# Gated mix of linear attention and a squared-ReLU network: the query weights folded in the first block, as 32 by 32 array tiles, and kept in DRAM until the second half

## The chip, the cores and the metric

The kernel runs on one core of a Trainium2 chip (trn2). The metric is the device time of one execution in microseconds; times given are medians of several runs. In the profile PE is the matrix engine TensorE (PEld its weight loads), DVE is VectorE, ACT is ScalarE, POOL is GpSimd and SP is SyncE, which only issues DMA transfers. PSUM has eight banks of 128 partitions x 512 float32 values; PE writes its products there.

## The reference

An input x of 2048 rows and 512 columns goes through two branches, mixed by a gate for each row:

```python
g = sigmoid((x * gate_w).sum(-1, keepdims=True))
q, k, v = split(x @ wqkv)                       # 32 heads of 16 columns
pq, pk = q @ w_phi[h], k @ w_phi[h]             # for each head h: 16 x 16
phi(p) = concat(softmax(p), softmax(-p))        # 32 features a head
kv, z = phi(pk).T @ v, phi(pk).sum(rows)
a = (phi(pq) @ kv) / (phi(pq) @ z + 1e-6) @ wo  # attention branch
h = relu(x @ w1 + b1) ** 2                      # 1792 hidden columns
b = h @ w2 + b2
out = g * a + (1 - g) * b
```

Since `q @ w_phi` is linear in x, the kernel multiplies the query weights with the heads' w_phi first, once ("folds" them), and x with the folded weights. It does the same for the keys.

## The kernel before

**Products.** A float32 value is split into a high part in the format float32r and a low part, value minus high (`split`, L62: ACT copies the high part, L64, DVE subtracts, L67). A product of two such numbers takes three matmuls (`mm3`, L75 to L79: high x high on L77, low x high on L78, high x low on L79).

**Order of the work.** `work_list` runs over two halves of the hidden columns (sweep 0 and 1), in each over four blocks of 512 rows, in each over seven chunks of 128 hidden columns: 56 steps. A step makes u = w1 chunk x block for a later step (`up_step`; ACT reads u with its bias and ReLU on L418, squares it on L419 and splits it), and adds its own hidden chunk x w2 chunk into four banks d (`down`). Between these products everything else is placed by a table: `at(slot, f)` (L782 and L785 to L838) puts f at half step `slot`; step t holds the slots 2t to 2t + 1.5. Within a slot, `tc.issue_after` orders an instruction behind another one of its engine, and `tc.high_priority` lets an instruction go ahead of others in its engine's queue where its own inputs allow. The result is one fixed queue for each engine, which the engine works off in order.

**The key and value part (sweep 0).** `load_fold` (L143) loads w_phi and the four 128-row pieces of the key weights into tiles "row" (six buffers, shared with the rows for the gate). `tiles_fold` (L177) multiplies them at half step 5.5 with 32 by 32 tiles of the PE array into the four banks a, b, e and f; DVE turns these (L196), and ACT copies them beside the value weights. The joint weights (keys and values in one 512 x 1024 matrix) are made into the operands of a product scheme with seven products in place of eight (`joint`, L218): DVE makes the sums of weight blocks (L216), `operand` (L203) splits them. Operands 2, 4, 5 and 7 (`HELD`) stay in SBUF, in tiles "wa" (2 and 4) and "wb"; 1, 6 and 3 (`KEPT`) are stored to DRAM by POOL (`wkeep`, L213) and loaded again by ACT's queue for each use (L635). Operand 4 is made last, at half step 14.5 (`joint_last`). Pairs of row chunks go through `block` (L637, matmuls on L647 to L649) from half step 14 on, with sums of blocks of x that DVE and POOL make (`sums_add`, L605).

**PSUM.** u, q, num, att and the folds take their banks from a list (`bank`, L51): the one used longest ago first. It holds a, b, e and f at the start. Bank b leaves the list at half step 6 (in `do_joint`) and holds the sum kv later; e leaves it at half step 14 for the pairs.

**The query weights before.** At half step 49 `do_wT(wqT)` loads w_phi (again) and the four pieces of query weights, 256 KB each (L145, L147). At half steps 53 to 56 `do_fold` makes one 128 x 512 piece k of the folded weights each (`fold`, L150): four float32 matmuls of 128 x 128 x 128 (L154) into one bank, which ACT and DVE split into the tiles "wa". They are due at 56.5, when the first query chunk is projected (`do_q`).

**Gate.** `gate_load` and `gate_chunk` (L259 to L268) load x by rows (L263) and have DVE sum x times gate_w for each row; for block 0 the loads stand at half steps 5.5, 5.5, 7.5 and 9.5, the chunks three half steps later.

Of the kernel before, what the change touches and what calls it, by code (L numbers as in the profile page):

```python
# [35 lines left out]
def tile_gated_mix(ctx: ExitStack, tc: tile.TileContext, xT, xn, wqT, wkT, wphi, wv, wo, w1, b1, w2, b2, gw, out):  # L36
# [96 lines left out]
    wkeep = dram.tile([len(KEPT), 2, P, 2 * D], F32, name="wkeep")  # L133
    zrow = dram.tile([2 * D], F32, name="zrow")
# [8 lines left out]
    def load_fold(wT):  # L143
        t = [row() for _ in range(1 + NK)]
        nc.sync.dma_start(t[0], wphi)  # L145
        for g in range(NK):
            nc.sync.dma_start(t[g + 1], wT[:, g, :])  # L147
        return t

    def fold(loaded, nm, k):  # L150
        wph, *t = loaded
        ps = bank(f"fold{nm}{k}")
        for g in range(NK):
            nc.tensor.matmul(ps[:, g * P:(g + 1) * P], t[g][:, k * P:(k + 1) * P], wph[:, g * P:(g + 1) * P],  # L154
                             start=True, stop=True)
# [47 lines left out]
    def operand(i, j, src, slot=None, ehi=None, elo=None):  # L203
        if i in HELD:
            w, k = "ab"[i > 4], 2 * (HELD.index(i) % 2) + j
            hi, lo = (wpool.tile([P, 512], F32R, tag=f"w{w}{hl}{k}", name=f"w{i}{j}", bufs=1) for hl in "hl")
        else:
            t = st["slots"][slot] if slot is not None else work.tile([P, 2 * D], F32R, tag="tb", name="spare", bufs=2)
            hi, lo = both(t)
        split(src, hi, lo, ehi or nc.scalar, elo or nc.vector)  # L210
        st["W"][i, j] = hi, lo
        if i in KEPT:
            st["stored"] = nc.gpsimd.dma_start(wkeep[KEPT.index(i), j], t.bitcast(F32))  # L213
# [45 lines left out]
    def gate_load(n):  # L259
        eng, pin = ((nc.sync, "in" if n > 1 else "wv"), (nc.gpsimd, "summed"), (nc.sync, "ahead"), (nc.sync, "ahead"))[n // NC]  # L260
        st["xn", n] = row()
        with tc.issue_after(st[pin].ins):
            st["xrow"] = eng.dma_start(st["xn", n], xn[n])  # L263
# [191 lines left out]
    def do_fold(nm, k):  # L455
        with tc.issue_after(st["up"].ins):
            st["wa", nm, k] = fold(st["wT"], nm, k)
        if k == NK - 1:
            st["wa"] = [st["wa", nm, i] for i in range(NK)]
            if nm == "k":  # L460
                banks.pop()
# [328 lines left out]
    for slot, j, piece in ((5.5, 0, 0), (6, 1, 0), (8, 0, 1), (9, 1, 1), (10, 1, 2), (11, 0, 2)):  # L790
        at(slot, do_joint, j, piece)
    for j in range(2):
        at(14.5, joint_last, j)
    for b in range(NB):
        for c in range(NC):
            s = b * SL + 2.5 * c - 1 if b > 1 else 17.5 + c / 2 if b else max(5.5, 3.5 + 2 * c)
            if b != 1 or c < 2:
                at(s, gate_load, b * NC + c)
            at(s + (4.5 if b == 1 else 3), gate_chunk, b * NC + c)
        if c == NC - 1:  # L800
            at(s + 4.5 if b == 1 else s + 3, gates, b)
# [7 lines left out]
    at(49, do_wT, wqT)  # L809
    for k in range(NK):  # L810
        at(53 + k, do_fold, "q", k)
# [137 lines left out]
```

## Time and profile before

| | |
|---|---|
| time, median of 3 runs | 508.11 us (507.98 to 508.29) |
| span of the profiled execution | 506.8 us |
| part of the median outside that span | 1.3 us |
| PE busy | 502.0 us, 99% |
| DVE, ACT, POOL busy | 405.9, 256.2, 88.4 us |
| moved by DMA | 76.13 MB |

The profile is that of one execution. Busy time counts an engine's instructions but not its waits; a row of a timeline gives the start, the duration, the engine, the line, the operation with its output and inputs, and in brackets the idle time ahead of it and what ended that. A matmul of 512 columns shows as 0.39 us, but the next one starts 0.227 us after it, since they are pipelined. A float32 matmul leaves two records, so sixteen instructions are x32.

### The profile page before, as it was taken

To read this page: it belongs to the slowest core of one execution; us is meant where nothing else is said; L and a number is where in the kernel's file an instruction comes from. 1 tells how busy PE (TensorE), PEld (TensorE's weight loads), DVE (VectorE), ACT (ScalarE), POOL (GpSimd) and SP (SyncE) were. 2 spreads that over 40 slices of the span, in tenths; PEclk is the share of its full clock that TensorE was granted. 3 is DMA by queue.
4 is the path that set the end of the run, shared out by engine and by line. 5 is a ranking of instruction groups with operands and counts; after the bars stand their busy time and mean duration, and the time that the engine had idled before them with its cause. 6 is when DMAs were issued, how large, how long until landed. Compare 5 with 4: busy or idle time off the path is not lost.

```text
span 506.8 us, 9362 instructions
## 1 busy us (share of the span) xinstructions
PE 502.0 (99%) x3522; PEld 406.4 (80%) x3522; DVE 405.9 (80%) x679; ACT 256.2 (51%) x458; POOL 88.4 (17%) x103
## 2 busy tenths in 40 slices
PE   9999999999999999999999999999999999999997
PEld 5878788788888888888888877788787878788776
DVE  5569957998795979796898989897869797897824
ACT  4887655555263474454574745444456354333540
POOL 0000151204420025000013050211222221111200
PEclk9999999999999999999999999999999999999999
DMA  8858587756854578771375221325112231032102
GB/s 262 279 194 284 187 311 219 232 196 231 288 187 158 182 236 308 242 228 65 87 219 195 63 83 43 104 76 147 39 31 88 71 85 43 8 125 63 38 26 84
DMA packets 45861, 76.13 MB, mean 150 GB/s; under 512 B 6904, under 2 KB 23032, under 8 KB 45816
## 3 DMA queue, kind: packets, MB, share of 16 engines
q1 hardware_dynamic: 36104, 41.78, 26.7%
q10 hardware_dynamic: 6768, 23.79, 13.7%
q0 software_dynamic: 2944, 9.96, 5.4%
q8 instruction: 28, 0.46, 0.4%
q14 instruction: 17, 0.14, 0.1%
HBM read 57.68 MB, written 11.54 MB: 137 GB/s over the span
## 4 chain that ended last, share of the span: by engine, by line
PE 90%; DVE 6%; DMA 1%; POOL 1%; ACT 1%; issue 1%; DVEq 0%; POOLq 0%; ACTq 0%
PE d L77 9%; PE d L78 9%; PE d L79 9%; PE u L77 9%; PE u L78 8%; PE u L79 8%; PE pX L647 3%; PE att L79 3%; PE pX L649 3%; PE att L77 3%; PE att L78 3%; PE pX L648 3%; PE q L79 2%; PE q L78 2%; PE q L77 2%; PE pY L647 2%
## 5 line engine op out<-in xcount | busy, mean ns | idle before, releaser
L418 ACT ACTIVATE r<-u,b1c 128x512 f32<-128x512 f32 x56 | 38.5, 688 | 125.5 <-PE u L79 123.6
L77 PE MATMUL d<-w2h,hh 128*128 128x512 f32 x222 | 86.9, 391 | 0.0
L78 PE MATMUL d<-w2l,hh 128*128 128x512 f32 x222 | 86.5, 390 | 0.0
L79 PE MATMUL d<-w2h,hl 128*128 128x512 f32 x222 | 86.4, 389 | 0.0
L77 PE MATMUL u<-xh,w1h 128*128 128x512 f32 x212 | 83.7, 395 | 0.0
L78 PE MATMUL u<-xl,w1h 128*128 128x512 f32 x212 | 82.6, 390 | 0.0
L79 PE MATMUL u<-xh,w1l 128*128 128x512 f32 x212 | 82.5, 389 | 0.0
L333 POOL TENSOR_TENSOR ez<-e,z 128x512 f32<-128x512 f32 x32 | 43.1, 1370 | 166.6 <-ACT e L305 166.6
L67 DVE TENSOR_TENSOR hl<-r,hh 128x512 fp32r<-128x512 f32 x56 | 37.7, 674 | 24.7 <-ACT hh L64 24.7
L77 PEld LDWEIGHTS d<-w2h,hh 128*128 128x128 f32 x222 | 41.7, 188 | 9.2 <-issue 0.6
L78 PEld LDWEIGHTS d<-w2l,hh 128*128 128x128 f32 x222 | 41.7, 188 | 8.9 <-DVE w2l L67 0.4
L77 PEld LDWEIGHTS u<-xh,w1h 128*128 128x128 f32 x212 | 39.8, 188 | 11.1 <-issue 2.9
L79 PEld LDWEIGHTS d<-w2h,hl 128*128 128x128 f32 x222 | 41.7, 188 | 8.7
L79 PEld LDWEIGHTS u<-xh,w1l 128*128 128x128 f32 x212 | 39.8, 188 | 8.6 <-DVE w1l L67 0.2
L78 PEld LDWEIGHTS u<-xl,w1h 128*128 128x128 f32 x212 | 39.8, 188 | 7.9
L305 ACT ACTIVATE e<-e 128x1024 f32<-128x1024 f32 x27 | 28.6, 1059 | 25.2 <-DVE e L303 25.0
L308 DVE TENSOR_REDUCE sm<-e 128x64 f32<-128x1024 f32 x27 | 32.8, 1214 | 10.4 <-ACT e L305 10.4
L64 ACT ACTIVATE hh<-r 128x512 fp32r<-128x512 f32 x56 | 35.2, 628 | 1.1
L419 ACT ACTIVATE r<-r 128x512 f32<-128x512 f32 x56 | 35.0, 624 | 0.7
L686 ACT ACTIVATE tmp<-pX 128x512 f32<-128x512 f32 x24 | 14.4, 598 | 31.2 <-PE pX L649 27.6
L371 ACT ACTIVATE phiT<-tb 32x256 f32<-32x256 f32 x64 | 26.4, 412 | 6.1 <-DVE tb L356 5.1
L340 DVE TENSOR_REDUCE dz<-ez 128x64 f32<-128x1024 f32 x16 | 19.4, 1211 | 11.5 <-POOL ez L333 11.5
(184 smaller groups left out, 985.5 us busy)
## 6 DMA issues: line engine op xcount, KB each, us to landing
sloto<-wkeep ACTq DMA_DIRECT2D x30, 512.0 KB, 4.1
in<-in_xT SPq DMA_DIRECT2D x42, 256.0 KB, 4.2
slotez<-wkeep ACTq DMA_DIRECT2D x15, 512.0 KB, 4.6
phiT<-tb SPq DMA_DIRECT2D x192, 32.0 KB, 1.9
in<-in_w SPq DMA_DIRECT2D x23, 256.0 KB, 3.2
part<-row POOLq DMA_DIRECT2D x16, 256.0 KB, 5.2
row<-part SPq DMA_DIRECT2D x16, 256.0 KB, 2.7
out<-row SPq DMA_DIRECT2D x15, 256.0 KB, 2.2
```

The costliest lines, as they stand in the source:

```text
L64: i = nc.scalar.activation(hi, src, AF.Copy)
L67: st["lo"] = elo.tensor_tensor(lo, src, hi.bitcast(F32), ALU.subtract)
L77: nc.tensor.matmul(o, ah[:, sa], bh[:, sb], start=first, stop=False)
L78: nc.tensor.matmul(o, ah[:, sa], bl[:, sb], start=False, stop=False)
L79: return nc.tensor.matmul(o, al[:, sa], bh[:, sb], start=False, stop=last)
L305: nc.scalar.activation(ef, ef, AF.Exp)
L308: nc.vector.tensor_reduce(sm, e3, AX.X, ALU.add)
L333: nc.gpsimd.tensor_tensor(ez[:, hs, :], e3[:, hs, :], zbc[half], ALU.mult)
L371: nc.scalar.activation(dst, src, AF.Copy)
L418: st["relu"] = nc.scalar.activation(r, ps, AF.Relu, bias=b1c[:, fc:fc + 1])
L419: nc.scalar.activation(r, r, AF.Square)
L647: nc.tensor.matmul(ps, h, wh, start=first and j == 0, stop=False, skip_group_check=True)
```

## The change

The query weights are loaded and folded in the first block, beside the key weights' work, and the folded weights, turned by DVE, are kept in DRAM until the second half.

- At half step 5.5 the four pieces of query weights are loaded (the tile with w_phi is kept from the key fold). The first gate load of block 0 stands behind them on SP's queue, the other three at 9.5, the gate chunks at 8.5, 12, 12.5 and 13.
- At 9.5 `query_fold` multiplies with sixteen matmuls, each on one 32 by 32 tile of the array over 512 columns, in all four banks a, b, e and f; each reads a 32-row strip of w_phi and of the query weights. DVE turns each bank with one instruction into the tile "turned", which shares its memory with the held operand 4. Bank b leaves the list here, no longer at 6.
- At 11.5 `query_store` stores the turned weights with four DMAs of POOL to `wfold` in DRAM, in runs of 512 bytes.
- At 49 `query_load` loads four plain 128 x 512 rows from there, and at 53 to 56 `query_split` splits one of them each. The sixteen matmuls of 128 x 128 x 128 are gone.

```diff
     def load_fold(wT):
-        t = [row() for _ in range(1 + NK)]
-        nc.sync.dma_start(t[0], wphi)
+        t = [row() for _ in range(NK)]
+        if "wph" not in st:
+            st["wph"] = row()
+            nc.sync.dma_start(st["wph"], wphi)
         for g in range(NK):
-            nc.sync.dma_start(t[g + 1], wT[:, g, :])
-        return t
-
-    def fold(loaded, nm, k):
-        wph, *t = loaded
-        ps = bank(f"fold{nm}{k}")
+            st["wqT"] = nc.sync.dma_start(t[g], wT[:, g, :])
+        return [st["wph"], *t]
+
+    def held(k):
+        if k < 2:
+            return [wpool.tile([P, 512], F32R, tag=f"wa{hl}{k}", name=f"wa{hl}{k}", bufs=1) for hl in "hl"]
+        if k == 2:
+            st["wa23"] = wpool.tile([P, 4, 512], F32R, tag="wa23", name="wa23", bufs=1)
+        return [st["wa23"][:, 2 * (k - 2) + i, :] for i in range(2)]
+
+    def query_fold():
+        wph, *t = st["wT"]
+        pss = [bank(f"fold{r}") for r in range(4)]
         for g in range(NK):
-            nc.tensor.matmul(ps[:, g * P:(g + 1) * P], t[g][:, k * P:(k + 1) * P], wph[:, g * P:(g + 1) * P],
-                             start=True, stop=True)
-        hi = wpool.tile([P, 512], F32R, tag=f"wah{k}", name=f"w{nm}h{k}")
-        lo = wpool.tile([P, 512], F32R, tag=f"wal{k}", name=f"w{nm}l{k}")
-        with tc.high_priority(offset=AHEAD):
-            split(ps, hi, lo, nc.scalar, nc.vector)
-        return hi, lo
+            for r in range(4):
+                rows = slice(32 * r, 32 * r + 32)
+                with tc.issue_after(st["up"].ins):
+                    st["up"] = nc.tensor.matmul(pss[r][32 * g:32 * g + 32, :],
+                                                wph[rows, g * P + 32 * r:g * P + 32 * r + 32], t[g][rows, :],
+                                                start=True, stop=True, skip_group_check=True)
+        tb = st["qrows"] = wpool.tile([P, 4 * NK, 4, 32], F32, tag="wa23", name="turned", bufs=1)
+        for r in range(4):
+            with tc.high_priority(offset=AHEAD):
+                st["qturned"] = nc.vector.transpose(tb[:, :, r, :], pss[r].rearrange("p (k q) -> p k q", q=32))
+        banks.remove(ps_b)
+
+    def query_store():
+        to = wfold.rearrange("t (c q) (g f) -> g q (t c) f", c=4, g=NK)
+        for g in range(NK):
+            with tc.issue_after(st["stored"].ins):
+                nc.gpsimd.dma_start(to[g], st["qrows"][32 * g:32 * g + 32].rearrange("p k r f -> p k (r f)"))
+
+    def query_load():
+        st["wq"] = [row() for _ in range(NK)]
+        for k in range(NK):
+            nc.sync.dma_start(st["wq"][k], wfold[k])
+
+    def query_split(k):
+        hi, lo = held(k)
+        with tc.issue_after(st["up"].ins), tc.high_priority(offset=AHEAD):
+            split(st["wq"][k], hi, lo, nc.scalar, nc.vector)
+        st.setdefault("wa", []).append((hi, lo))
...
-        eng, pin = ((nc.sync, "in" if n > 1 else "wv"), (nc.gpsimd, "summed"), (nc.sync, "ahead"), (nc.sync, "ahead"))[n // NC]
+        eng, pin = ((nc.sync, "wqT"), (nc.gpsimd, "summed"), (nc.sync, "ahead"), (nc.sync, "ahead"))[n // NC]
         st["xn", n] = row()
-        with tc.issue_after(st[pin].ins):
+        with tc.issue_after(st[pin].ins), tc.high_priority(offset=AHEAD) if n < NC else nullcontext():
...
-        if (j, piece) == (1, 0):
-            banks.remove(ps_b)
...
+    at(5.5, do_wT, wqT)
+    at(9.5, query_fold)
+    at(11.5, query_store)
...
-    at(49, do_wT, wqT)
+    at(49, query_load)
     for k in range(NK):
-        at(53 + k, do_fold, "q", k)
+        at(53 + k, query_split, k)
```

`operand` takes the tiles of operands 2 and 4 from `held` now; nothing else of it changes. Line numbers behind the new functions are larger by 24 to 34: the sums of weight blocks on L216 are L250 after the change, the new matmuls are on L167 and the turns on L173.

Where this lands in the queues is shown at three places. The first is PE at half step 9.5, before: the last products d of the step (d_307 to d_309 are three of the four d banks), and behind them the first of the next u.

```order
L79 MATMUL d_307<-w2h_332,hl 128x512
L77 MATMUL d_308<-w2h_332,hh 128x512
L78 MATMUL d_308<-w2l_333,hh 128x512
L79 MATMUL d_308<-w2h_332,hl 128x512
L77 MATMUL d_309<-w2h_332,hh 128x512
L78 MATMUL d_309<-w2l_333,hh 128x512
L79 MATMUL d_309<-w2h_332,hl 128x512
L77 MATMUL u<-xh_0_526,w1h_130 128x512
```

The same place after (the same d banks are now d_308 to d_310, fold_632 to fold_635 are the four banks of the fold). The last four of the sixteen fold matmuls are shown; twelve like them stand ahead, right behind the product that was the first row above.

```order
L167 MATMUL fold_632<-row 32x512
L167 MATMUL fold_633<-row 32x512
L167 MATMUL fold_634<-row 32x512
L167 MATMUL fold_635<-row 32x512
L77 MATMUL d_309<-w2h_333,hh 128x512
L78 MATMUL d_309<-w2l_334,hh 128x512
L79 MATMUL d_309<-w2h_333,hl 128x512
L77 MATMUL d_310<-w2h_333,hh 128x512
L78 MATMUL d_310<-w2l_334,hh 128x512
L79 MATMUL d_310<-w2h_333,hl 128x512
L77 MATMUL u<-xh_0_533,w1h_131 128x512
L78 MATMUL u<-xl_0_534,w1h_131 128x512
```

The fold comes in between the d products; six d products stay between it and the next u, whose bank is that of fold_632.

The second place is DVE at the same time, before: low parts of operands (sloto, w) and of w2, and sums of weight blocks (raw, tmp).

```order
L67 TENSOR_TENSOR sloto_396<-tmp,sloto_396 128x512
L216 TENSOR_TENSOR raw_398<-raw_400,raw_398 128x512
L216 TENSOR_TENSOR tmp<-tmp 128x512
L67 TENSOR_TENSOR w2l_557<-in,w2h_556 128x512
L216 TENSOR_TENSOR tmp<-tmp 128x512
L67 TENSOR_TENSOR w_583<-raw_398,w_582 128x512
```

After:

```order
L67 TENSOR_TENSOR sloto_397<-tmp,sloto_397 128x512
L250 TENSOR_TENSOR raw_399<-raw_401,raw_399 128x512
L250 TENSOR_TENSOR tmp<-tmp 128x512
L173 STREAM_TRANSPOSE turned<-fold_632 128x16x32
L173 STREAM_TRANSPOSE turned<-fold_633 128x16x32
L173 STREAM_TRANSPOSE turned<-fold_634 128x16x32
L173 STREAM_TRANSPOSE turned<-fold_635 128x16x32
L250 TENSOR_TENSOR tmp<-tmp 128x512
L67 TENSOR_TENSOR w2l_564<-in,w2h_563 128x512
L67 TENSOR_TENSOR w_588<-raw_399,w_587 128x512
```

The four turns stand behind two sums and ahead of the low part of w2.

The third place is PE between half steps 53 and 56, at the second of the four old folds (foldq), before:

```order
L77 MATMUL d_2355<-w2h_384,hh 128x512
L78 MATMUL d_2355<-w2l_385,hh 128x512
L79 MATMUL d_2355<-w2h_384,hl 128x512
L154 MATMUL foldq_2989<-row 128x128 x4
L77 MATMUL u<-xh_0_2041,w1h_2486 128x512
L78 MATMUL u<-xl_0_2042,w1h_2486 128x512
```

After, with the same d bank now d_2390:

```order
L77 MATMUL d_2390<-w2h_385,hh 128x512
L78 MATMUL d_2390<-w2l_386,hh 128x512
L79 MATMUL d_2390<-w2h_385,hl 128x512
L77 MATMUL u<-xh_0_2076,w1h_2521 128x512
L78 MATMUL u<-xl_0_2077,w1h_2521 128x512
```

The four matmuls are gone here and at the other three places; the u products follow the d products directly.

More of the change, by code (lines that the diff above doesn't have):

```diff
@@ L133, in tile_gated_mix @@
     wkeep = dram.tile([len(KEPT), 2, P, 2 * D], F32, name="wkeep")
+    wfold = dram.tile([NK, P, D], F32, name="wfold")
     zrow = dram.tile([2 * D], F32, name="zrow")
@@ L204, in operand @@
         if i in HELD:
-            w, k = "ab"[i > 4], 2 * (HELD.index(i) % 2) + j
-            hi, lo = (wpool.tile([P, 512], F32R, tag=f"w{w}{hl}{k}", name=f"w{i}{j}", bufs=1) for hl in "hl")
+            k = 2 * (HELD.index(i) % 2) + j
+            if i > 4:
+                hi, lo = (wpool.tile([P, 512], F32R, tag=f"wb{hl}{k}", name=f"w{i}{j}", bufs=1) for hl in "hl")
+            else:
+                hi, lo = held(k)
         else:
@@ L453, in do_wT @@
         st["wT"] = load_fold(wT)
[L455 to L461, printed above, removed]
     def do_joint(j, piece):
```

7 lines of the change are left out of this document (4 added, 3 removed).

## Prediction

> **What bounds the kernel now.** I read the page first, then the chain of work that ended last, the groups of instructions by form, and the timelines of PE, DVE, ACT and SP around half step 9.5, where the change puts its work, and around 53 to 56, where it takes work away. From the page:
>
> ```profile
> span 506.8 us, 9362 instructions
> PE 502.0 (99%) x3522; PEld 406.4 (80%) x3522; DVE 405.9 (80%) x679; ACT 256.2 (51%) x458; POOL 88.4 (17%) x103
> PEclk9999999999999999999999999999999999999999
> PE 90%; DVE 6%; DMA 1%; POOL 1%; ACT 1%; issue 1%; DVEq 0%; POOLq 0%; ACTq 0%
> ```
>
> PE is busy for 502.0 of 506.8 us at full granted clock, and the chain runs over PE for 90%. So each microsecond that PE is spared shortens the run, and each one that PE is made to wait lengthens it, unless a wait of PE further on shrinks by as much. The stretches of ten microseconds in which the new work lands look the same; the columns are PE, PEld, DVE, ACT and POOL busy, PE clock, DMA share and KB per us:
>
> ```profile
> 36.00:46.00 10.00, 10.00 (x45) 7.93 (x44) 8.92 (x18) 8.43 (x16) 2.21 (x4) 1.00 0.92 293
> 46.00:56.00 10.00, 10.00 (x46) 8.29 (x45) 10.00 (x20) 6.95 (x13) 1.06 (x2) 1.00 0.49 187
> ```
>
> PE has no gap there, but DVE is nearly full too (8.92, then 10.00 of 10 us). This is where DVE gets four more instructions that PE will wait for.
>
> **Removed: four folds on PE.** In the chain they stand as four pieces at half steps 53 to 56:
>
> ```profile
> 245.55 0.89 PE foldq L154 x8
> 250.63 0.89 PE foldq L154 x8
> 254.25 0.89 PE foldq L154 x8
> 257.88 0.89 PE foldq L154 x8
> ```
>
> All four lie on PE's path with nothing beside them: 4 x 0.89 = 3.56 us less. ACT and DVE still make the four high and low parts there, now from rows in SBUF rather than from PSUM; the count of instructions is the same, the weights are first needed at half step 56.5, and no wait of PE hung on them. I cost this at nothing. The gate chunks of block 0 move by a few half steps; their gates are due only when block 0 ends, and I cost that at nothing too.
>
> **Added on PE: the fold at half step 9.5.** No row shows sixteen 32x32 tiles over 512 columns, so I bound it by the two nearest forms:
>
> ```profile
> L183 PE MATMUL fold<-row 32*32 32x128 f32 x128 | 1.9, 278 | 0.0
> 27.07 1.83 PE fold L183 x104
> 489.94 1.02 PE num L382 x32
> L196 DVE STREAM_TRANSPOSE turned<-fold 128x512 f32<-128x512 f32 x4 | 2.5, 684 | 0.4 <-PE fold L183 0.4
> ```
>
> The key fold has 128 records of 128 columns in 1.83 us. The numerator has 32 records of 256 columns on eight tiles, four records to a tile: 1024 columns in a tile's turn in 1.02 us. The new fold has 16 instructions, 32 records (the old folds too left two records for each instruction), two to a tile, so 2 x 512 = 1024 columns as well. I take 1.0 us from the numerator, which has the same length of run, with 1.8 as the upper end. The size matters little, as the next term shows.
>
> **Added: PE waits for VectorE.** The fold takes all four PSUM banks that the u products rotate through. Where PE stands now:
>
> ```profile
> 39.84 0.39 PE L79 MATMUL d<-w2h,hl 128*128 128x512 f32 x1
> 40.07 0.39 PE L77 MATMUL d<-w2h,hh 128*128 128x512 f32 x1
> 41.43 0.39 PE L77 MATMUL u<-xh,w1h 128*128 128x512 f32 x1
> ```
>
> The fold comes in ahead of the d product of 40.07. Six d products (six starts of 0.227 us, 40.07 to 41.43) follow it, and then the next u, whose bank is the one that the fold filled first. PE can start this u only when DVE has turned that bank. The fold's fourth bank waits in turn for ACT to have read the last u. Here is ACT, then DVE:
>
> ```profile
> 40.63 0.67 ACT L418 ACTIVATE r<-u,b1c 128x512 f32<-128x512 f32 x1
> 42.31 0.63 ACT L64 ACTIVATE w2h<-in 128x512 fp32r<-128x512 f32 x1 [1.01 <-DMA in<-in_w]
> 42.85 0.62 ACT L64 ACTIVATE sloto<-tmp 128x512 fp32r<-128x512 f32 x1
> ```
>
> ```profile
> 43.50 0.69 DVE L67 TENSOR_TENSOR sloto<-tmp,sloto 128x512 fp32r<-128x512 f32 x1 [0.84 <-ACT sloto L64]
> 44.10 0.68 DVE L216 TENSOR_TENSOR raw<-raw,raw 128x512 f32<-128x512 f32 x1
> 44.71 0.69 DVE L216 TENSOR_TENSOR tmp<-tmp 128x512 f32<-128x512 f32 x1
> 45.31 0.69 DVE L67 TENSOR_TENSOR w2l<-in,w2h 128x512 fp32r<-128x512 f32 x1
> ```
>
> ACT frees the fourth bank at 40.63 + 0.67 = 41.30, so the fold ends near 42.4 and the six d near 43.8. But by the order of the program the first turn stands on DVE where the low part of w2 stands now, that is at 45.31. It cannot come sooner, though it is of high priority: ahead of it on DVE is the low part of the slot (43.50), which waits for ACT's high part (42.85), which stands behind the w2 split (42.31), which waits for a load. DVE goes through its queue in order. The first turn thus ends at 45.31 + 0.68 = 46.0, and u starts at about 46.05 in place of 41.43: **4.6 us more on PE**. Any fold that ends by 44.6 (3.3 us past 41.3) gives the same, so its own 1.0 to 1.8 us is hidden. Behind the waiting u on PE stand all further products; behind the turns on DVE stand the low part of w2 and the rest of the weight sums, 4 x 0.61 = 2.4 us later (0.61 is the step from one start to the next in the rows above), but PE, their reader, is 4.6 us later by then.
>
> Bounds on this term. The load that starts the queue is issued late, because its buffer comes free late:
>
> ```profile
> 32.00 5.16 SPq L87 DMA_DIRECT2D in<-in_w  x3
> 36.83 0.33 SPq L87 DMA_DIRECT2D in<-in_w  x1
> 37.25 1.43 SPq L263 DMA_DIRECT2D row<-in_xn  x2
> ```
>
> It is issued at 36.83 and lands at about 42.3, 5.5 us in a full DMA stretch (share 0.92). The two gate loads right behind it go elsewhere with the change; if that lets it land a microsecond sooner, ACT and DVE are a microsecond sooner and the term is 3.6. Upward: the turn writes 16 strips of 32 with gaps between them, and were it to take twice the 0.68 us of a plain one, the term is 5.3.
>
> By the Trainium skill's page "TensorEngine Tiling (Array Packing)", section PSUM Bottleneck, tiling speeds up the products but not the emptying of PSUM, which may then be what limits. That speaks against this change, and the rows agree: 2.5 us for four turns against 1.83 us for the fold. Were the emptying's own pace the limit, u would wait for one turn right behind the fold, 42.4 + 0.7, under the six d products, and the sum would be the quick rival's below; it is the place in DVE's queue that I go by.
>
> **Given back.** Two waits of PE on the chain, for ACT's and DVE's sums of block pairs, go:
>
> ```profile
> 58.14 0.34 PE pX L647
> 58.94 0.42 PE pX L649
> PEld pX L649 <- DVE sl L67: 0.4, 1, 0.4
> PEld pX L647 <- ACT sh L64: 0.3, 1, 0.3
> ```
>
> Their steps are 0.11 and 0.19 us longer than the usual 0.23. PE comes 4.6 us later and DVE 2.4 us later, so DVE and ACT are in time: 0.3 us less.
>
> **Loads and stores.** The four rows of query weights (1.05 MB) go out at about 29, when the key rows have been read, ahead of the w1 and w2 loads of 32.0:
>
> ```profile
> 26.00:36.00 10.00, 10.00 (x165) 8.03 (x164) 5.47 (x9) 8.38 (x26) 0.10 (x1) 1.00 0.57 194
> 30.00:35.00 5.00, 5.00 (x24) 4.14 (x23) 2.66 (x6) 4.65 (x19) 0.00 (x0) 1.00 0.41 151
> in<-in_w SPq DMA_DIRECT2D x4, 256.0 KB, 2.8
> row<-in_wqT SPq DMA_DIRECT2D x4, 256.0 KB, 4.3
> ```
>
> At a full share 194 KB per us becomes 194 / 0.57 = 340, so 1.05 MB is 3.1 us of all DMA engines, and 30 to 35 has 59% of 5 us free, 2.95 us. So the loads nearly fit: I cost them at 0, with 0.75 us as the end if the w loads land a microsecond later. The query rows themselves have till 40 to land, and took 4.3 us each at half step 49. The plain loads at half step 49 replace others of the same size on the same queue, one fewer: nothing.
>
> **The sum.** -3.56 + 4.6 - 0.3 = +0.75, so 506.8 becomes 507.6 in the span. The median of the runs stands 1.3 us above the profiled span; I keep that: **508.9 us**, within 0.2% (1.0 us, about what a measurement of this kernel can tell from no change) of 508.11. The forecast's own range: with 3.6 for the wait, 508.11 - 0.26 = 507.8; with 5.3 for it, 0.75 for the loads and nothing given back, 508.11 - 3.56 + 6.05 = 510.6.
>
> **The rivals.**
> Quick: the turns don't hold PE. That is so if DVE has turned the first bank by about 43.8, when the six d are through, 2.2 us sooner than I have it. Then PE pays the fold and its wait for ACT's bank only: 42.4 - 40.07 = 2.3 at most, 1.0 at least, so -3.56 + 1.0 to 2.3, 505.5 to 506.9, say 506.3. For it: DVE stands 0.84 us idle at 43.5 and ACT 1.01 us at 42.3, both for a load. Against: both idle times together are less than the 2.2 us needed, and three 0.61 us instructions stand between. Chance 0.16.
>
> Loads in the way: the query rows push the w loads back by more than the free 2.95 us, PE waits for w1 or w2 at 33 to 38 and DVE is later besides. Loads of 256 KB that took 2.8 us in the median would take 5.5 as the one at 36.83 does, so 2.7 us late at most; part of it hides in the wait that PE has anyway. 508.9 + 1 to 2.7, say 510.7. Chance 0.08.
>
> Stores that hold ACT (this ends slower): the tile of turned rows has the memory of one held operand, which ACT writes at half step 14.5. The four stores stand on POOL behind the last kept slot. The rows below are POOL's store of that slot, ACT's u of the time, the time to landing of the block-sum loads, and that of the stores of whole rows:
>
> ```profile
> 54.13 0.53 POOL L213 DMA_DIRECT2D wkeep<-slotez  x1 [1.28 <-DVE slotez L67]
> 67.84 0.69 ACT L418 ACTIVATE r<-u,b1c 128x512 f32<-128x512 f32 x1 [2.25 <-PE u L79]
> DMA to landing us min/median/max: 3.9/5.7/5.7
> part<-row POOLq DMA_DIRECT2D x16, 256.0 KB, 5.2
> ```
>
> The slot's store would come at about 54.1 + 2.4 = 56.5, the four issues (0.53 each) be through by 59.2, and ACT want the memory after the u of 67.84, about 71 to 72 with the delay. So the stores have some 12 us. Loads of block sums, whose runs are 512 bytes like these, took 5.7 us at most; stores of whole rows 5.2. From 12 us on ACT stands, and with it the reading of the u and pX banks that PE waits for, up to one for one: at 16 us, 508.9 + 4 = 512.9. Twice the slowest row is under the point where it begins, so chance 0.05. In the Trainium skill, "DMA: Bandwidth & Descriptors", section Specifications, 512 bytes is the smallest transfer at full line rate; these runs just reach it, which would leave this rival out.
>
> Tiles that don't run at once: the fold is hidden up to 3.3 us. At the old folds' pace, 0.89 / 8 = 0.11 us for 128 columns, 32 records of 512 columns one after another take 14 us, 10.9 more than is hidden: 519.8. The key fold's 1.83 us for 128 such tiles speaks against it. Chance 0.03.
>
> **How the numbers follow.** The forecast's mechanism has the remaining 0.68. Of its range, 507.8 to 509.1 is within 0.2% and 509.1 to 510.6 above; I give 0.42 and 0.26, since the point lies at 508.9. Faster by over 0.2%: 0.16, the quick rival. Slower: 0.26 + 0.08 + 0.05 + 0.03 = 0.42. Same: 0.42. The range reaches into both sides: from 506.4, which leaves out about half of the quick rival (0.08), to 510.7, which leaves out the last two rivals and half of the loads (0.12).
>
> **What would show it.** Right: the key line is u's first product behind the new fold, waiting about 2.3 us for DVE's turn, with the fold's fourth bank waiting about 1 us for ACT; u starts at 46 us, the chain passes there from PE to DVE; the four 0.89 us pieces are gone at 245 to 258; no wait on ACT for stores before the operand at 70. Wrong: u starts by 44.5 (quick), or PE shows a wait for w1h or w2h between 33 and 39 (loads), or ACT's copy behind 67 waits for a DMA (stores), or the fold's row is over 3.3 us (tiles).

## The result and the profile after

The changed kernel takes 515.51 us (median of 4 runs, 513.41 to 516.66) where before takes 508.08 (4 runs): a ratio of 1.0142, 95% interval 1.0129 to 1.0155, 7.4 us slower by the medians. The forecast was 508.9 and its range ended at 510.7, so it was wrong: it saw the wait for the turned bank, and missed most of the time. The profiled execution is the shortest of the four, 513.41 us with a granted clock of 1.000; the other three had a clock of 0.995 to 0.996 and took 515.4 to 516.7. So there are two things to explain: 4.8 us in the span (511.6 against 506.8), and the 2.0 to 3.3 us more of the other three executions.

The page of after, its span, busy times and chain:

```profile
span 511.6 us, 9388 instructions
PE 500.9 (98%) x3522; PEld 403.5 (79%) x3522; DVE 406.8 (80%) x683; ACT 257.0 (50%) x458; POOL 90.6 (18%) x107
PE 81%; DVE 10%; DMA 4%; issue 2%; POOL 1%; ACT 1%; SPq 0%; DVEq 0%; POOLq 0%; ACTq 0%
```

PE is busy for 1.1 us less than before, in a longer span, and its share of the chain went from 90% to 81%: PE waits now. What PE waited for (us in total, times, longest), in a kernel that had only 0.18 us of such waits behind its start:

```profile
PE pX L671 <- DMA sloto<-wkeep: 2.4, 1, 2.4
PE u L77 <- DVE turned L173: 1.4, 1, 1.4
PE u L77 <- ACT w1h L64: 1.2, 1, 1.2
PE att L79 <- DVE o L67: 0.8, 1, 0.8
```

Only the second of these four was a term of the forecast's sum. Where they stand on PE, with the fold between them:

```profile
38.03 0.50 PE L77 MATMUL u<-xh,w1h 128*128 128x512 f32 x1 [1.21 <-ACT w1h L64]
41.68 1.75 PE L167 MATMUL fold<-row 32*32 32x512 f32 x32
46.46 0.50 PE L77 MATMUL u<-xh,w1h 128*128 128x512 f32 x1 [1.44 <-DVE turned L173]
66.18 0.50 PE L671 MATMUL pX<-sloto,sh 128*128 128x512 f32 x1 [2.43 <-DMA sloto<-wkeep]
```

The turns on DVE's timeline, and on ACT's the split that waits for w2's load:

```profile
45.70 2.50 DVE L173 STREAM_TRANSPOSE turned<-fold 128x512 f32<-128x512 f32 x4
```

```profile
36.71 0.63 ACT L64 ACTIVATE w2h<-in 128x512 fp32r<-128x512 f32 x1 [1.11 <-DMA in<-in_w]
```

The first turn starts at 45.70 (45.31 forecast) and u at 46.46 (46.05 forecast). To see what each stretch costs, take the start of the same product in both traces; the difference is how late PE is (products whose place in PE's order changed are left out):

| place in after, us | PE later than before, us | what was added there |
|---|---|---|
| 38.0 (u behind the w1 wait) | 1.55 | w1's load behind the query rows |
| 43.4 (d behind the fold) | 3.3 | the fold and its wait for ACT |
| 46.5 (u behind the turn) | 5.0 | the wait for DVE |
| 63.4 (pX) | 4.5 | 0.5 given back |
| 66.2 (pX on the reloaded slot) | 7.0 | a reload |
| 242 | 7.4 | |
| 273 | 3.7 | the four old folds, 3.6, are gone |
| 325, and to the end | 4.6 | a wait for o |

The last two rows belong together. o is the attention's numerator of the first query chunks, and its low part stands in DVE's queue behind steps that need POOL's products with z, the sum of the key features. The first of these products starts at 267.84 in before and waits for ACT there. After the change it starts 5.71 us later and waits for z, which goes through DRAM:

```profile
273.55 2.53 POOL L367 TENSOR_TENSOR ez<-e,z 128x512 f32<-128x512 f32 x2 [8.40 <-DMA z<-zrow]
```

### The profile page after: what moved, and what is told of

The parts are those of the page before. It is cut to its first block, busy times and chain, and to the rows that moved or that the text cites. A ratio compares the mean times of both kernels' runs of the same rounds, so it can differ in the third digit from the quotient of the medians.

```text
span 511.6 us, 9388 instructions
## 1 busy us (share of the span) xinstructions
PE 500.9 (98%) x3522; PEld 403.5 (79%) x3522; DVE 406.8 (80%) x683; ACT 257.0 (50%) x458; POOL 90.6 (18%) x107
## 4 chain that ended last, share of the span: by engine, by line
PE 81%; DVE 10%; DMA 4%; issue 2%; POOL 1%; ACT 1%; SPq 0%; DVEq 0%; POOLq 0%; ACTq 0%
PE d L78 8%; PE d L77 8%; PE d L79 8%; PE u L77 7%; PE u L79 7%; PE u L78 7%; PE pX L671 3%; PE att L79 3%; PE att L77 3%; PE att L78 3%; PE pX L673 3%; PE pX L672 3%; PE q L79 2%; PE q L78 2%; PE q L77 2%; PE pY L673 2%
```

## The experiments

Each was compared with before in runs of its own on the same chip; a median is followed by its difference from that of before beside it. Medians of different chips are compared by these differences. A trace is one execution, and executions of one kernel differ: in the traces here PE is between 0.5 us ahead of before's and 0.2 us behind at 12 us, where no edit has done anything yet.

**The changed kernel again.** No edit.

> The changed kernel as it is, run again beside the others. Ledger theory: the profiled span is again near 511.6 us, 4.8 above before, made up of 1.4 (w1's load behind the query rows) + 1.75 (fold) + 1.7 (turn) - 0.5 (waits given back) + 2.9 (a reload of a kept operand behind the stores of the folded weights) - 3.6 (old folds) + 0.7 (a wait for o at 310 us). Executions with a granted clock under 1.000 are some 2 us longer. Rival: the waits differ from execution to execution, and the profiled one is not typical; then other waits stand in this trace.

514.81 us (+6.0; ratio 1.0133, 1.0101 to 1.0165), clocks 0.993 to 1.000. The same waits stand in its trace: 2.5 us for the reload, 1.8 for the turn, 1.0 for w1. They belong to the kernel, not to one execution. But the profiled one took 513.5 us in the span, 1.8 more than the first, with a clock of 1.00 for as long as PE had products; it has a wait of 1.0 us for the features of a chunk and one of 0.8 us that the profile explains by nothing ("issue"), which the first didn't have. So a lower clock is not the only thing that makes executions differ.

**The stores earlier.**

```diff
-    at(11.5, query_store)
+    at(9.5, query_store)
```

> The four stores of the folded weights stand on POOL ahead of the last two kept slots, so they go at 48 to 52 us, when the DMA engines are nearly idle. Ledger theory: PE's wait of 2.4 us for the reload at 58 to 66 us goes, and the time falls by 2.0 to 2.9 us. Rival (the reload is late because VectorE, and so the stores of the two kept slots, are 2.8 us later): the wait stays, since those two stores come no sooner, and the time falls by less than 0.5 us.

513.16 us (+4.4; ratio 1.0098, 1.0078 to 1.0118), 1.65 less than the changed kernel beside it; the two intervals overlap a little, so it is the trace that decides. First the changed kernel: POOL's stores of the last two kept slots and of the folded weights, then the piece of its chain for the reload that ACT issued at 58.35, and the landing times of the four stores.

```profile
55.09 0.53 POOL L247 DMA_DIRECT2D wkeep<-spare  x1 [9.69 <-DVE spare L67]
55.69 0.53 POOL L247 DMA_DIRECT2D wkeep<-slotez  x1
56.22 2.63 POOL L180 DMA_DIRECT2D wfold<-turned  x4
```

```profile
58.35 7.79 DMA sloto<-wkeep
```

```profile
DMA to landing us min/median/max: 5.0/6.8/8.1
```

2 MB of stores start between 55.1 and 58.9, and the reload of 512 KB right behind them is 7.8 us under way, 4.1 in the median of before. With the four stores at 48 us, PE's waits are:

```profile
PE u L77 <- DVE turned L173: 1.6, 1, 1.6
PE pX L671 <- DMA sloto<-wkeep: 0.3, 1, 0.3
```

The reload's wait is gone, though the two stores of kept slots come as late as ever (54.9 and 55.5). It is the folded weights' stores that hold the reload. The gain in the median is a little under the 2.0 us expected.

**The loads behind w1 and w2.**

```diff
         for g in range(NK):
-            st["wqT"] = nc.sync.dma_start(t[g], wT[:, g, :])
+            with tc.issue_after(st["in"].ins) if "in" in st else nullcontext():
+                st["wqT"] = nc.sync.dma_start(t[g], wT[:, g, :])
...
-    at(5.5, do_wT, wqT)
+    at(6.5, do_wT, wqT)
```

> The four loads of query weights stand on SP behind the loads of w1 and w2 of that step, no longer ahead of them. Ledger theory: PE's wait of 1.2 us for w1 at 38 us goes, but as PE then stands longer at the turn (VectorE is only some 0.5 us sooner), the time falls by only 0.4 to 0.9 us. Rival (the whole queue of ACT and VectorE is late by that load): the turn comes 1.2 us sooner as well and the time falls by 1.2 us or more.

518.79 us (+10.0): worse by 4, which neither theory had. The wait for w1 is gone, but ACT stands at the next thing that shares the DMA engines with the query rows, the store of a kept slot, whose memory ACT wants to write; PE then waits for ACT and longer for the turn:

```profile
42.21 0.63 ACT L64 ACTIVATE sloto<-raw 128x512 fp32r<-128x512 f32 x1 [2.63 <-DMA wkeep<-sloto]
```

```profile
PE fold L168 <- ACT r L453: 2.2, 1, 2.2
PE u L77 <- DVE turned L174: 1.9, 1, 1.9
```

And the granted clock falls behind these waits. The columns are the stretch, PE, PEld, DVE, ACT, POOL, PE clock, DMA share, KB per us:

```profile
46.00:48.00 2.00, 0.19 (x1) 0.00 (x0) 2.00 (x5) 2.00 (x4) 0.53 (x1) 1.00 0.99 331
48.00:50.00 2.00, 1.95 (x7) 1.56 (x8) 2.00 (x4) 0.18 (x1) 0.00 (x0) 0.78 0.72 290
50.00:52.00 2.00, 2.00 (x6) 1.58 (x5) 2.00 (x4) 0.63 (x1) 0.00 (x0) 0.50 0.02 6
52.00:54.00 2.00, 2.00 (x9) 1.57 (x8) 2.00 (x5) 1.26 (x2) 0.00 (x0) 0.87 0.47 133
```

Behind the idle stretch the clock is at one half for 3.4 us (49.1 to 52.5), and once more for 3.4 us at 69.6, behind a wait of 2.2 us for the reload. Three of the four executions have a mean clock of 0.993 and took 518.5 to 519.5 us; the one with 1.000 took 515.23. So two such falls cost 3.3 to 4.3 us here, and without them the edit is about as slow as the changed kernel. This is the second half of the result.

**The fold in two halves.** Two banks at a time, so that the u between them has a bank that needs no turn.

```diff
-        pss = [bank(f"fold{r}") for r in range(4)]
+        two = (2 * half, 2 * half + 1)
+        pss = {r: bank(f"fold{r}") for r in two}
...
-    at(9.5, query_fold)
+    at(9.5, query_fold, 0)
+    at(10.5, query_fold, 1)
```

> The fold is cut in two: row strips 0 and 1 into two banks at half step 9.5, strips 2 and 3 into two banks at 10.5, so that the u between them has a bank that needs no turn. Ledger theory: PE's wait for the turn (1.4 us) and for ACT's read of the last bank (0.4 us) goes, the time falls by 1.5 to 1.9 us, less what the second switch to small tiles costs. Rival (the waits only move: the u after next needs the first half's bank, and VectorE is as late there): the time falls by under 0.5 us. Rival (switching the array to small tiles and back is what costs): the fold's two pieces take longer together than the one piece of 1.75 us, and the time rises or stays.

516.16 us (+7.4), no better. At its place it did what it should: each half takes 1.09 us on PE, no wait for the turn is left, and PE is 2.4 us late at 50 us, not 5.2; 0.7 us of that difference was there at 12 us already, so the halves gain about 2.0. But the reload takes it all back, and the clock goes down behind that:

```profile
PE pX L675 <- DMA sloto<-wkeep: 3.9, 1, 3.9
```

```profile
66.00:68.00 2.00, 2.00 (x7) 1.55 (x6) 0.75 (x1) 1.14 (x2) 0.00 (x0) 0.54 0.93 363
68.00:70.00 2.00, 2.00 (x7) 1.59 (x6) 0.00 (x0) 0.00 (x0) 1.68 (x3) 0.60 0.88 328
```

**Both.** Halves, and the stores pinned behind the store that stood last before the fold, at 10.5.

> Both edits that helped at their own place at once: the fold in two halves (PE is 2.3 us late behind it in place of 5.1), and the stores of the folded weights in the idle stretch before the last kept slots. Ledger theory: with the reload no longer late, the halves' 2.75 us are kept, so the profiled span is 511.0 (stores early alone) - 2.75 = 508.3 us, 1.0 to 1.8 above before, and the granted clock is 1.00 in all executions, since no wait of PE over 1.5 us is left. Rival (another fixed point, such as the gate or the sums of row blocks, holds PE at about 70 us as the reload did): over 510 us.

512.4 us (+4.6; span 509.0, clocks 0.999 to 1.000). That is better than the halves alone (+7.4), but no better than the stores earlier alone (+4.4); the profiled execution, 510.82, is the shortest of four. PE still waits 2.1 us for the reload: the pin moved only the first two of the four stores ahead of the kept slots (48.4), the other two went at 54.3, and the reload was 6.9 us under way.

**Without the query loads.** As the last, with `at(5.5, do_wT, wqT)` taken out.

> The kernel of the halves with early stores, without the four loads of query weights: the fold reads the key rows again, so the query branch gets wrong weights. It prices the loads in the first block. Ledger theory: PE's waits between 33 and 40 us go and the span falls by 0.3 to 1.3 us against the halves with early stores. Rival (the loads cost nothing once the turn isn't waited for): within 0.2 us of it.

511.78 us (+4.0; span 508.7). PE is 0.55 us less late at 50 us, and 0.04 us less at the end. In these two traces the loads have a price at their place, and it is hidden later.

**Before without its folds.**

```diff
-        ps = bank(f"fold{nm}{k}")
-        for g in range(NK):
-            nc.tensor.matmul(ps[:, g * P:(g + 1) * P], t[g][:, k * P:(k + 1) * P], wph[:, g * P:(g + 1) * P],
-                             start=True, stop=True)
+        ps = t[k]
```

> The kernel before with its four folds left out: the query rows are split as they were loaded, so the query branch gets unfolded weights. It measures the most that taking the folds from there can bring. Both theories of the forecast: 3.56 us less than before, 503.2 to 503.8 in the profiled span if before is 507.0. Rival (DVE or POOL sets the time around 250 to 310 us, so part of it is given back): 2 to 3 us less.

505.36 us (-2.4; ratio 0.994, 0.9921 to 0.9959). That is 2.1 to 4.0 us less by the interval, which doesn't leave out the 3.56; the trace does, for its execution: PE is 3.57 us early at 296 us and 2.52 at 325, so one microsecond of the removed folds is worth nothing there. Here is POOL's first product with z and the first attended product that waits, for before, then without the folds:

```profile
267.84 2.53 POOL L333 TENSOR_TENSOR ez<-e,z 128x512 f32<-128x512 f32 x2 [4.18 <-ACT e L305]
305.82 0.50 PE L79 MATMUL att<-woh,o 128*128 128x512 f32 x1 [0.18 <-DVE o L67]
```

```profile
265.31 2.54 POOL L330 TENSOR_TENSOR ez<-e,z 128x512 f32<-128x512 f32 x2 [7.19 <-DMA z<-zrow]
303.30 0.50 PE L79 MATMUL att<-woh,o 128*128 128x512 f32 x1 [1.23 <-DVE o L67]
```

POOL's product moves by 2.53 us and the attended product by 2.52: from there on DVE and POOL set the pace, and POOL now waits for z, which is summed by PE right behind the first of the four folds and then goes through DRAM. Three of the four folds stood behind that point, so leaving them out doesn't bring z.

**The same with z from elsewhere.** z is read from the gate weights, an input.

```diff
-            nc.sync.dma_start(z, zrow[half * D:(half + 1) * D].partition_broadcast(P))
+            nc.sync.dma_start(z, gw.partition_broadcast(P))
```

> The kernel before without its four folds, as tried, and with z read from an input that lies in DRAM from the start, in place of the one that is written at the end of the key and value part (so the query weights and the denominators are wrong). Theory (of the 3.56 us, 1.0 is given back because z goes through DRAM at 260 to 265 us and the first chunks of queries wait for it): the wait of 1.2 us for o at 303 us falls to about 0.2, and the span is 1 us shorter than without the folds alone. Rival (VectorE's own work between 265 and 303 us sets that point): the wait and the time stay.

504.18 us (-3.9; ratio 0.9914, 0.9886 to 0.9942), span 502.6, and PE has no wait for o any more. POOL's first product with z starts at 264.27, 3.57 us earlier than in before and not 2.53. So z is what takes back that microsecond. The intervals of the two kernels overlap, so this too rests on the traces; and a little of the gain in this one has another reason, told under "All four stores first".

**The key fold's form, late.** In before, at 53 and 54, each time 32 matmuls into two banks, turned by DVE and split from there.

```diff
+        for g in range(NK):
+            for c in range(4):
+                for r in two:
...
+                        st["up"] = nc.tensor.matmul(pss[r][cols, g * P:(g + 1) * P],
...
-        at(53 + k, do_fold, "q", k)
+        at((54.5, 55, 55.5, 56)[k], q_split, k)
+    for half in range(2):
+        at(53 + half, q_tiles, half)
```

> The kernel before, with the folds at half steps 53 and 54 in the key fold's form: 32 matmuls of 32 by 32 tiles over 128 columns into two banks each time, turned by VectorE and split from there, nothing in the first block and nothing through DRAM. Theory (such small matmuls go by their count, 128 records in 1.83 us): two pieces of 0.92 us in place of four of 0.89, 1.7 us less than before. Rival (they go by the columns of one tile, as the halves of the new fold did, 1.05 us each where the whole took 1.75): two pieces of some 1.8 us, and the time stays. Rival (VectorE's four turns and eight half splits there hold the first query chunk): slower by 1 us or more.

510.65 us (+2.9). On PE the pieces of the chain are

```profile
245.46 1.08 PE fold L464 x64
250.91 0.44 PE fold L464 x17
251.43 0.92 PE fold L464 x47
```

that is 2.44 us in place of 3.56, and PE is 0.6 us early at 296 us. Then comes its longest wait:

```profile
PE num L382 <- DMA phiT<-tb: 3.0, 1, 3.0
```

The numerator waits for the first chunk's features. It is z again: DVE's turns and half splits stand ahead of its last copy of the sums of z, which starts at 262.66 (the last two ran at 254.88 to 255.74 in before), and POOL's first product with z starts at 272.39, 4.55 us later than in before. The second of the two rivals was right.

**All four stores first.** Halves, with `do_joint(1, 2)` at 10.5 behind the stores and the kept slots' stores pinned behind them, so that all four are on POOL ahead of the last two kept slots.

> The fold in two halves, and all four stores of the folded weights ahead of the last two kept slots (with the halves and early stores before, two of the four still stood behind one of them, and the reload was 6.9 us under way and PE 2.1 us late). Ledger theory: the reload is no longer waited for, the span falls by 2.1 us against that kernel, to 506.5 to 507.3, 0 to 1 us above before; the granted clock stays at 1.000. Rival (the 1 MB of stores delays the reload wherever it stands): the wait stays over 1.5 us.

512.29 us (+4.2; span of the profiled execution 510.5). The reload's wait is gone, as expected, and yet nothing is gained. PE is 0.7 us late at 273 to 296 us, then 3.4 at 325. Its longest wait is now

```profile
PE att L79 <- DVE o L67: 1.8, 1, 1.8
```

PE was 4.3 us late when z was summed, and POOL's first product with z starts at 271.24, 3.40 us later than in before; the folds that PE no longer does afterwards don't help z. But that alone doesn't tell why the kernel called "Both" does better in its trace: there this product comes at 270.93, 3.09 us late, and PE is only 1.96 us late at the end. The rest is decided by two instructions that start within 10 ns of each other, the first of POOL's fourth pair of products with z and one that stands ahead of o in DVE's queue. Here they are in before, in the changed kernel, in this kernel and in "Both":

```profile
300.13 1.29 POOL L333 TENSOR_TENSOR ez<-e,z 128x512 f32<-128x512 f32 x1 [5.79 <-ACT e L305]
300.14 2.36 DVE L314 TENSOR_TENSOR e<-e,w 128x1024 f32<-128x1024 f32 x1
```

```profile
305.86 2.38 POOL L367 TENSOR_TENSOR ez<-e,z 128x512 f32<-128x512 f32 x1 [5.80 <-ACT e L339]
305.86 1.22 DVE L348 TENSOR_TENSOR e<-e,w 128x1024 f32<-128x1024 f32 x1
```

```profile
303.53 1.30 POOL L373 TENSOR_TENSOR ez<-e,z 128x512 f32<-128x512 f32 x1 [5.79 <-ACT e L345]
303.54 2.37 DVE L354 TENSOR_TENSOR e<-e,w 128x1024 f32<-128x1024 f32 x1
```

```profile
303.23 1.23 DVE L353 TENSOR_TENSOR e<-e,w 128x1024 f32<-128x1024 f32 x1
303.23 2.38 POOL L372 TENSOR_TENSOR ez<-e,z 128x512 f32<-128x512 f32 x1 [5.80 <-ACT e L344]
```

One of the two takes about 1.1 us longer, and it matters to o only if it is DVE's. With that, the end can be worked out from z: PE's lateness at the end is that of POOL's first product with z, less 1.14 us where DVE's instruction is the short one. For the changed kernel 5.71 - 1.14 = 4.57 (4.6 measured), for "Both" 3.09 - 1.14 = 1.95 (1.96), here 3.40 (3.4), and it holds within 0.05 us in ten of the thirteen traces; in the other three (the key fold's form late, z from elsewhere, one wait alone) PE is not held there, or the two don't start together. No run sets which of the two is the long one. It explains two earlier results: without the folds DVE's was the long one, with z from elsewhere the short one.

**Long runs.** The changed kernel, the four stores written in runs of 8 KB.

> The changed kernel with the four stores at their place, but written to DRAM in runs of 8 KB as they stand in SBUF (the blocks are not put back in order, so the query weights are wrong). Same bytes, other runs. Theory of the run length (DMA share over 1.0 while only 160 KB per us move): the stores are through some 3 us sooner, PE's wait of 2.4 us for the reload falls to under 0.5 us and the time by 2 us or more. Theory of the amount: 1 MB takes its time in any form, and the wait stays at 1.5 us or more.

515.98 us (+7.9). The reload is 7.70 us under way and PE waits 2.3 us, behind which the clock is at one half for 3.4 us. The run length makes no difference; the bytes in front of the reload do.

**One wait, alone.** Before, with five small memsets on POOL at 45 us and one small matmul that reads them.

```diff
+    def fill():
+        for _ in range(5):
+            with tc.issue_after(st["stored"].ins):
+                nc.gpsimd.memset(scratch, 0.0)
+
+    def stall():
+        z = scratch.bitcast(mybir.dt.bfloat16)
+        with tc.issue_after(st["up"].ins):
+            st["stall"] = st["up"] = nc.tensor.matmul(bank("stall")[:, :128], z[:, :P], z, start=True, stop=True)
...
+    at(9.5, fill)
+    at(10.5, stall)
```

> The kernel before with one wait of PE put in and nothing else: five small memsets on POOL behind the store of a kept slot (45 us), and one small matmul of PE at half step 10.5 that reads what they wrote. PE gets there at about 42.8 us and waits some 2.5 us. Theory without the clock: 2.5 us, less the 0.3 to 0.5 us of later waits of PE that vanish, 2.0 to 2.4 us more in every execution, granted clock 1.000. Theory of the clock (a wait of 2 us and more lets the granted clock fall to one half for some 4 us in some executions): in part of the executions a granted clock of 0.993 to 0.997 and another 1.5 to 2.5 us, so they spread over 510 to 513 us, where those of before spread by 1 us.

512.37 us (+4.1; six runs, 511.06 to 513.96, clocks 0.993 to 1.000, where the eleven of before lie between 507.33 and 508.80 with clocks of 0.999 and 1.000). PE waited 3.4 us, longer than planned. The profiled execution, its matmuls and its clock:

```profile
46.09 0.23 PE L484 MATMUL stall<-scratch 128*128 128x128 bf16 x1 [3.41 <-POOL scratch L479]
47.66 0.63 PE L79 MATMUL u<-xh,w1l 128*128 128x512 f32 x1
48.08 0.63 PE L77 MATMUL d<-w2h,hh 128*128 128x512 f32 x1
48.51 0.63 PE L78 MATMUL d<-w2l,hh 128*128 128x512 f32 x1
```

```profile
44.00:46.00 2.00, 0.00 (x0) 0.00 (x0) 2.00 (x5) 1.97 (x5) 1.27 (x6) 1.00 1.13 359
46.00:48.00 2.00, 1.91 (x7) 1.57 (x8) 2.00 (x5) 0.86 (x2) 0.04 (x1) 0.76 0.99 382
48.00:50.00 2.00, 2.00 (x6) 1.53 (x5) 2.00 (x4) 1.68 (x3) 0.00 (x0) 0.50 0.43 118
50.00:52.00 2.00, 2.00 (x9) 1.61 (x9) 2.00 (x5) 1.20 (x3) 0.00 (x0) 0.89 0.00 0
```

From 47.2 to 50.2 us a matmul starts 0.43 us after the one before, not 0.227; the clock is at one half from 47.0 to 50.5. Apart from the wait, the kernel has only the small matmul with its bank more, and the order that keeps it in its place, so the wait is what lowers the clock, and not in every execution. PE is 3.4 us late when the clock falls and 5.1 when it is back: 1.6 us for one fall. Later waits of before that vanish give 1.3 us back.

## Why the prediction was wrong

Three steps failed, the first of them the largest: the stores were put at nothing although they hold a reload (2.5 to 3.0 us); "no wait of PE hung on" the folds, although z and the first query chunks did (0.9 us here, and it could have been 2.0); and the full granted clock was taken for granted (1.6 us for a fall, in some executions). The wait for the turned bank, the forecast's own mechanism, is there.

**Removed: 3.56 us.** Right on PE (3.6 in the trace), wrong at the end. The step that failed here is "no wait of PE hung on them. I cost this at nothing". The chain of z and the first query chunks, which stopped PE for 0.18 us before, stops it for 0.8 us after. PE is 7.4 us late when z is summed and 4.6 at the end, so 2.8 of the 3.6 us arrive, and 1.14 of these are luck: DVE's instruction at 305.86 was the short one, where it was the long one in before. Alone, the folds are worth 2.4 us in the median; that z takes back the rest is shown by the traces without the folds, and then with z from elsewhere.

**Added: the fold and the turn, 4.6 us.** Nearly right: 5.0 us at that u, 46.46 against 46.05. The split differs. By the table, 1.55 us for w1 came first, then 1.75 for the fold with its wait for ACT, then 1.7 for the turn. As forecast, the place of the turn in DVE's queue sets it. But DVE doesn't get there as forecast: the load that was to hold the queue is in time (no wait in the row below, where before has 1.01 us), and DVE works without a gap from 39.06 to the turn, late behind the w1 and w2 loads of before that. That the turn still came within 0.4 us of the forecast is in part luck.

```profile
42.37 0.63 ACT L64 ACTIVATE w2h<-in 128x512 fp32r<-128x512 f32 x1
```

A half of the fold takes 1.09 us on eight tiles, near the 1.0 that the numerator, on eight tiles too, gave for the whole; the whole takes 1.75 with its wait for ACT inside, and what it takes without that wait no run shows.

**Loads: 0, at most 0.75.** PE waited 1.2 us for w1, since ACT could split w2 only at 36.71 and w1 at 37.35, behind the load, where before had 35.29 and 35.81. The w loads stand behind the query rows in SP's queue; they were issued 0.2 us later than before and took 4.5 us to land instead of 2.8, so the free DMA time of 30 to 35 us, right as a sum, was not free for them. With that came what the prediction named as the sign of its rival "loads in the way", a wait for w1h between 33 and 39. In the sum it cost at most the 0.4 us by which the turn came later than forecast, because the wait for the turn is counted from DVE's time.

**Given back: 0.3 us.** 0.5 in the trace.

**The stores: 0, and a rival of 0.05 by way of ACT.** This is the term that was missing, 2.5 to 3.0 us, and the step that failed first. The rival looked for a victim among those who wait for the stores themselves, and gave them 12 us; they landed in 8.1 at most and nobody waited for them. The victim is a transfer that doesn't depend on them at all, but shares the DMA engines: the reload that ACT issues at 58.35, while the last of these stores goes out. Its row was on the page, 4.1 us in the median, and before's timelines had it and its product:

```profile
55.30 0.33 ACTq L635 DMA_DIRECT2D sloto<-wkeep  x1
```

```profile
59.20 0.40 PE L647 MATMUL pX<-sloto,sh 128*128 128x512 f32 x1
```

It landed 3.5 us after its issue there, 0.4 us ahead of the product. After the change PE comes 4.5 us later, but the reload is issued 3.05 us later too, behind a kept slot's store that comes 2.8 us later (55.09 for 52.31). So it has 0.4 + 4.5 - 3.05 = 1.9 us to spare; 4.3 us more under way leave a wait of 2.4. The rule of the Trainium skill cited there, that runs of 512 bytes reach the full rate, agrees with the long runs (2.3 us of wait against 2.4), but it leaves out a rival by run length only, not one by bytes.

**The clock: not in the forecast.** "At full granted clock" was taken as a property of the kernel; it held there because PE hardly waited. The granted clock was 1.00 in all slices before, and falls to 0.50 for 3.4 us behind waits of 2.2 to 3.9 us in the traces with the loads behind, the halves, the key form late, the long runs and the one wait. Waits of 2.1 to 2.5 us in the two traces of the changed kernel, in "Both" and without the query loads were not followed by it, so it is a matter of the single execution. The profiled execution of the changed kernel escaped; the other three have a mean of 0.995 to 0.996, as the traces with one fall have (0.995 to 0.997). One fall costs 1.6 us, and they are longer by 2.0 to 3.3; what the rest is, no trace of them shows. DVE's instruction at 305.86, 1.14 us longer, would be of that size. In the Trainium skill, "TensorE: Matmul & The Clock Gate", Part 1, the clock goes to one half after an idle window of about 3.4 us and back after as long a busy one, and the window runs freely, so that the same kernel measures different numbers of slow matmuls. The half clock, its 3.4 us, and the scatter between executions agree with the rows above; but here single waits of 2.2 us (the reload, loads behind) and 2.3 us (the long runs) were enough.

So in the profiled execution: -3.6 + 5.0 - 0.5 + 3.0 + 0.9 = 4.8, of which the forecast had -3.56 + 4.6 - 0.3. The two missing terms are waits at places that the change doesn't touch, 20 and 260 us further on. The 0.9 would be 5.71 - 3.73 = 2.0 had DVE's instruction been the long one.

## What to carry to other kernels

Work that is taken from a busy engine at one place is worth what the next fixed point behind it lets through: look for the first product that depends on a chain through other engines or DRAM (here z and the first o), read how much slack it has, and cap the gain by that. When transfers are moved into a stretch, list every transfer that is issued while they are under way, not only those who wait for them; the one with the least slack pays. And a wait of PE of two microseconds or more cost its own length and, in some executions here, another 1.6 us in half clock, so a change that trades steady work for one wait must win by more than the wait. Last, when two traces differ by a microsecond, look for a pair of instructions that start together before giving the difference to the edit.

## What the runs showed of the hardware

A 3.4 us wait of PE, alone, was followed by 0.43 us between matmul starts for 3.4 us in the profiled execution, and six executions with it spread over 2.9 us where eleven without it spread over 1.5. The same 3.4 us at half clock follow waits of 2.2 to 3.9 us in four other traces, and don't follow waits of 2.1 to 2.5 us in four. Stores of 1 MB in 512-byte or in 8 KB runs held a 512 KB reload on another queue equally, 7.8 and 7.7 us under way. Eight of sixteen tiles take 1.09 us for 16 records of 512 columns, all sixteen, with a short wait inside, 1.75 for 32. A product of two SBUF tiles on DVE (1.22 us) and one on POOL (1.29) that start within 10 ns of each other take 1.22 and 2.38 us, or 2.36 and 1.29.
